# Loading one weight matrix in a single transfer: w_in as one load of 56 KB per partition instead of two of 28 KB

## The chip, the cores and the metric

The kernel runs on one core of one Trainium2 chip. The metric is the device time of one execution in microseconds (us), the median over several executions. Executions of one kernel mostly agree within 0.5 us. Differences of a few tenths of a us are therefore at the edge of what can be seen.

## The reference, cut to what matters

A decode step mixes two branches by a sigmoid gate: an attention with a long cache (4 key/value heads, 65,536 positions, head size 128), and a small gated MLP (here `B`) on one token.

```python
x = A_x                                        # 1 x 1 x 1024
g = sigmoid((x * gate_w).sum(-1))
a = attention(x @ wq, k_cache, v_cache) @ wo   # k_cache, v_cache: 4 x 65536 x 128 each, bf16
z = gelu(x @ w_in)                             # w_in: 1024 x 3584
z1, z2 = z[:1792], layernorm(z[1792:])
b = (z1 * (w_sp * z2 + b_sp)) @ w_out          # w_sp, b_sp: one number each
out = g * a + (1 - g) * b
```

All weights and the cache are read once, 162 MB in bf16. `w_in` is 7.34 MB of that.

## The kernel before: what the change touches

All large loads go into one SBUF buffer, `kv`, of five slots of 32 KB per partition, and all are issued by SyncE on one queue, in the order of use. `load` issues one transfer into the slot `at`; a slot is loaded again when its readers have finished. The very first load is moved ahead of the start-up barrier by a helper that is left out here.

```python
P = 128; CT = 128; NKV = 5                      # slot: CT * P elements of bf16 = 32 KB per partition
kv = big.tile([P, NKV * CT * P], BF16, name="kv")

def load(src, shape, at):                       # at: slot number
    ...                                         # n: elements of one partition
    v = kv[:, int(at * CT * P):int(at * CT * P) + n]
    ...
    ins = nc.sync.dma_start(out=v, in_=src)
    return v

# four small loads on ScalarE's queue: x and gate_w (8 rows of 256 B each), w_sp, b_sp (2 B each)
nc.scalar.dma_start(out=xg8[:, 0, :], in_=A_x...)
nc.scalar.dma_start(out=xg8[:, 1, :], in_=gate_w...)
nc.scalar.dma_start(out=wb[:, 0:1], in_=B_w_sp)
nc.scalar.dma_start(out=wb[:, 1:2], in_=B_b_sp.unsqueeze(0))

KH = KC // 2                                    # KC = 8 rows of w_in and wq per partition
win_view = B_w_in.rearrange("(p c) n -> p c n", c=KC)
win_t = [load(win_view[:, i * KH:(i + 1) * KH, :], (KH, F), 3 + i) for i in range(2)]
wq_view = A_wq.rearrange("(p c) n -> p c n", c=KC)
wq_t = [load(wq_view[:, i * KH:(i + 1) * KH, :], (KH, HD), 1 - i) for i in range(2)]
...
# PE: xb_ps (x and gate to columns), small_ps (gate, w_sp, b_sp), then z, tot_ps, q:
for i in range(2):
    x_rows(z_ps, win_t[i], ZN, i)               # 32 matmuls 128x448 for each half
...                                             # DVE: gelu, layernorm sums -> tot_ps -> uT
for i in range(2):
    x_rows(q_ps, wq_t[i], HN, i)                # 32 matmuls 128x512 for each half
...                                             # DVE: q, build_w
build_w(0)
for j in range(NT):                             # first K tiles go to slots 2, 1, 0, 3
    k_tile(0, j, load_kv(A_k_cache, 0, j, (2, 1, 0, 3)[j])[0])
    ...
project(load(B_w_out..., (FC, D), 4), FC, uT, 0, first=True)
...                                             # K and V loads of 64 KB per partition, in turn
for j, n, at in ((0, 2, 1), (2, 1, 3), (3, 1, 4)):   # the last V loads
    ...
...                                             # wo in six loads, the last two of 2 KB per partition
```

On PE, z comes after `small_ps`, which waits for b_sp; and q comes after `tot_ps`, which waits for z's work on DVE. The trace shows PE keep to that order: w_in's first half had landed at 11.12 us, but z began at 12.66, after the `small_ps` matmuls on b_sp at 12.15. The K load into slot 1 waits for q's first half (done at 32.94 us, the issue at 32.99), the one into slot 0 for its second half.

## Time and profile before

| | before |
|---|---|
| median time | 383.22 us (383.17 to 383.25, 3 runs) |
| read | 162.0 MB, mean 425 GB/s |
| busy: PE, DVE | 61%, 57% of the span |
| packets of the load queue | 4324 |

From the page of the kernel before: the span, the busy time of the engines, the busy share of the DMA engines and their rate in 40 equal slices, the packets by queue (packets, MB, share of the span of 16 engines), and the chain that ended last by engine. (PE is TensorE's matmuls, PEld its weight loads, DVE VectorE, ACT ScalarE, POOL GpSimd, SP SyncE; a q after a name is the engine's sequencer, L167 is line 167 of the kernel, x32 a count of instructions. A slice of the span is 9.5 us long.)

```profile
span 381.4 us, 2581 instructions
PE 232.4 (61%) x1372; PEld 56.8 (15%) x796; DVE 218.4 (57%) x211; ACT 39.6 (10%) x55; POOL 4.4 (1%) x10
...
DMA  9999999999999999999999999999999999999995
GB/s 376 439 426 416 433 436 440 436 461 429 400 426 440 440 435 426 440 440 440 440 428 440 440 440 433 428 427 406 433 440 428 426 433 427 440 411 436 440 405 230
DMA packets 4375, 162.17 MB, mean 425 GB/s; under 512 B 520, under 2 KB 524, under 8 KB 908
...
q1 hardware_dynamic: 4324, 162.01, 98.7%
q8 instruction: 8, 0.13, 0.1%
...
DMA 59%; PE 20%; DVE 16%; issue 2%; ACT 1%; SPq 1%; DVEq 0%; ACTq 0%
```

The DMA engines are at 90% or more in every slice but the last. The load queue (q1) alone takes 98.7% of what 16 engines could give. No compute engine is near that. Note queue q8, whose kind is "instruction": eight instruction fetches of 16 KB (0.13 MB), counted as 0.1% of the same 16 engines; they come up again later.

The timeline of the load queue (start in us, duration of the issue, what is issued; the very first w_in load, at 0.00 us, lies before this window):

```profile
0.79 0.33 SPq L167 DMA_DIRECT2D kv<-in_B_w_in_dram  x1
1.16 0.97 SPq L167 DMA_DIRECT2D kv<-in_A_wq_dram  x2
6.87 0.33 SPq L167 DMA_DIRECT2D kv<-in_A_k_cache_dram  x1
32.99 0.33 SPq L167 DMA_DIRECT2D kv<-in_A_k_cache_dram  x1
42.77 0.81 SPq L167 DMA_DIRECT2D kv<-in_A_k_cache_dram  x2
```

And the timeline of the engines at the start (start, duration, engine, line, what, how often, and in brackets how long the engine was idle before and for whom):

```profile
9.13 0.37 PE L233 MATMUL xb_ps<-xg,spread 8*128 8x256 bf16 x1 [9.13 <-DMA xg<-in_gate_w_dram]
11.94 0.16 DVE L249 CAST wbf<-wb 1x2 f32<-1x2 bf16 x1 [1.00 <-DMA wb<-in_B_b_sp_dram]
12.66 3.17 PE L277 MATMUL z_ps<-kv,xT 128*32 128x448 bf16 x32
19.67 3.07 PE L277 MATMUL z_ps<-kv,xT 128*32 128x448 bf16 x32 [3.84 <-DMA kv<-in_B_w_in_dram]
27.57 0.56 PE L316 MATMUL tot_ps<-rs,ones_f 128*128 128x2 f32 x2 [4.83 <-DVE rs L314]
29.39 3.55 PE L277 MATMUL q_ps<-kv,xT 128*32 128x512 bf16 x32 [1.26 <-DMA kv<-in_A_wq_dram]
39.12 3.61 PE L277 MATMUL q_ps<-kv,xT 128*32 128x512 bf16 x32 [6.18 <-DMA kv<-in_A_wq_dram]
48.83 8.89 DVE L384 STREAM_TRANSPOSE kv<-kv 128x2048 int32<-128x2048 int32 x4 [1.59 <-DMA kv<-in_A_k_cache_dram]
59.84 2.31 DVE L384 STREAM_TRANSPOSE kv<-kv 128x2048 int32<-128x2048 int32 x1 [2.12 <-DMA kv<-in_A_k_cache_dram]
```

Read it from the bottom up: DVE waits for K, q waits for wq, z's second half waits for w_in. Each of them waits for the stream of loads. Three pieces of the chain of waits (start, duration, what) show how deep the queue is:

```profile
197.63 25.93 DMA kv<-in_A_k_cache_dram
...
347.00 31.88 DMA kv<-in_A_wo_dram
378.92 0.43 PE out_ps L478 x3
```

The K load issued at 197.63 us is 8.39 MB and needs 19 us at 440 GB/s, but it lands after 25.93 us: other loads are ahead of it (the last of them, a V load, landed at 204.19 us). The last output weights land at 378.88 us and only PE, ScalarE and the store of the result follow.

### The profile page before, as it was taken

The page shows a single profiled execution, that of the slowest core. Times are in us where ns is not written, and L with a number is a line of the kernel's source. Part 1 is how long each engine was busy: PE and PEld are TensorE (multiplying, and loading weights), DVE is VectorE, ACT ScalarE, POOL GpSimd, SP SyncE. Part 2 cuts the span into 40 slices and gives each one's busy share as a digit, 9 for nine tenths or more (in the row PEclk, how much of TensorE's full clock was granted, in tenths as well). Part 3 has the DMA queues.
Part 4 walks back from the last instruction along what each step waited for, and adds up shares of the span by engine and source line. Part 5 has one row for each costly group of instructions (what it writes and reads, how often), then busy time and mean ns, then how long its engine had stood idle before and what let it go on. Part 6 is the DMA issues. An engine that isn't in the chain of part 4 may idle for free.

```text
span 381.4 us, 2581 instructions
## 1 busy us (share of the span) xinstructions
PE 232.4 (61%) x1372; PEld 56.8 (15%) x796; DVE 218.4 (57%) x211; ACT 39.6 (10%) x55; POOL 4.4 (1%) x10
## 2 busy tenths in 40 slices
PE   0433467678157944796397629872967196849355
PEld 0110011112011210121011101120111011212123
DVE  4241487996687506966977059669780488550040
ACT  1010001111601100114010001050001010500000
POOL 4000000000000000000000000000000000000000
PEclk9966659998759895989588959895799679969766
DMA  9999999999999999999999999999999999999995
GB/s 376 439 426 416 433 436 440 436 461 429 400 426 440 440 435 426 440 440 440 440 428 440 440 440 433 428 427 406 433 440 428 426 433 427 440 411 436 440 405 230
DMA packets 4375, 162.17 MB, mean 425 GB/s; under 512 B 520, under 2 KB 524, under 8 KB 908
## 3 DMA queue, kind: packets, MB, share of 16 engines
q1 hardware_dynamic: 4324, 162.01, 98.7%
q8 instruction: 8, 0.13, 0.1%
q14 instruction: 3, 0.02, 0.0%
q10 hardware_dynamic: 40, 0.01, 0.0%
HBM read 162.01 MB, written 0.00 MB: 425 GB/s over the span
## 4 chain that ended last, share of the span: by engine, by line
DMA 59%; PE 20%; DVE 16%; issue 2%; ACT 1%; SPq 1%; DVEq 0%; ACTq 0%
DMA kv<-in_A_k_cache_dram 37%; PE s_ps L391 15%; DVE kv L384 9%; DMA kv<-in_A_wo_dram 8%; DMA kv<-in_A_wq_dram 7%; DMA kv<-in_A_v_cache_dram 7%; PE o_ps L437 3%; DVE pt L427 2%; DVE mx L386 1%; DVE o_sb L451 1%; PE q_ps L277 1%; ACT sc L424 1%; DVE rowt L447 1%; ACT sc L402 1%; SPq L167 1%
## 5 line engine op out<-in xcount | busy, mean ns | idle before, releaser
L391 PE MATMUL s_ps<-kv,wt 128*128 128x512 bf16 x512 | 142.1, 437 | 81.8 <-DVE kv L384 81.7
L384 DVE STREAM_TRANSPOSE kv<-kv 128x2048 int32<-128x2048 int32 x64 | 142.7, 2280 | 55.5 <-DMA kv<-in_A_k_cache_dram 55.5
L437 PE MATMUL o_ps<-kv,pt 128*64 128x512 bf16 x512 | 61.6, 399 | 7.7 <-DMA kv<-in_A_v_cache_dram 7.7
L391 PEld LDWEIGHTS <-wt 128*128 128x128 bf16 x256 | 27.5, 108 | 197.6 <-issue 140.2
L402 ACT CAST sc<-s_ps 128x1024 bf16<-128x1024 f32 x16 | 16.2, 1013 | 253.5 <-PE s_ps L391 253.5
L437 PEld LDWEIGHTS <-pt 128*64 128x64 bf16 x256 | 16.0, 115 | 50.7 <-issue 48.1
L427 DVE STREAM_TRANSPOSE pt<-sc 128x1024 bf16<-128x1024 bf16 x16 | 18.6, 1217 | 6.8 <-ACT sc L424 6.8
L386 DVE TENSOR_REDUCE mx<-sc 128x1 f32<-128x1024 bf16 x12 | 14.5, 1207 | 10.1 <-ACT sc L402 10.1
L424 ACT ACTIVATE sc<-sc,nb 128x1024 bf16<-128x1024 bf16 x16 | 18.2, 1137 | 12.2 <-DVE nb L420 12.2
L447 DVE TENSOR_TENSOR rowt<-o_ps,own 128x1024 f32<-128x1024 f32 x4 | 4.8, 1194 | 24.9 <-PE o_ps L437 24.9
L457 PE MATMUL om_ps<-o_sb,hsel 128*32 128x128 f32 x8 | 2.5, 421 | 19.7 <-DVE o_sb L451 19.7
L406 DVE TENSOR_REDUCE mx<-sc 128x1 f32<-128x1024 bf16 x4 | 4.9, 1220 | 14.2 <-ACT sc L402 14.2
L277 PE MATMUL q_ps<-kv,xT 128*32 128x512 bf16 x64 | 7.2, 627 | 7.4 <-DMA kv<-in_A_wq_dram 7.4
L478 PE MATMUL out_ps<-kv,oa 128*32 128x256 bf16 x128 | 6.7, 366 | 3.7 <-DMA kv<-in_A_wo_dram 2.2
L277 PE MATMUL z_ps<-kv,xT 128*32 128x448 bf16 x64 | 6.2, 570 | 3.8 <-DMA kv<-in_B_w_in_dram 3.8
L344 DVE TENSOR_TENSOR rowt<-q_ps,own_b 128x512 f32<-128x512 f32 x2 | 1.3, 686 | 12.5 <-PE q_ps L277 12.5
L451 DVE TENSOR_REDUCE o_sb<-rowt 128x128 f32<-128x1024 f32 x4 | 7.5, 1872 | 0.1
L292 DVE TENSOR_TENSOR rowt<-z_ps,own_b 128x448 f32<-128x448 f32 x2 | 1.2, 620 | 8.5 <-PE z_ps L277 8.5
L233 PE MATMUL xb_ps<-xg,spread 8*128 8x256 bf16 x1 | 0.4, 367 | 9.1 <-DMA xg<-in_gate_w_dram 9.1
L277 PEld LDWEIGHTS <-xT 128*32 128x32 bf16 x64 | 3.0, 139 | 19.4 <-issue 19.3
L478 PEld LDWEIGHTS <-oa 128*32 128x32 bf16 x128 | 4.4, 124 | 6.1 <-issue 3.3
L521 ACT CAST out_sb<-out_ps 128x256 bf16<-128x256 f32 x1 | 0.4, 372 | 45.4 <-PE out_ps L478 45.4
(88 smaller groups left out, 54.8 us busy)
## 6 DMA issues: line engine op xcount, KB each, us to landing
kv<-in_A_k_cache_dram SPq DMA_DIRECT2D x4, 4096.0 KB, 26.8
kv<-in_A_wq_dram SPq DMA_DIRECT2D x2, 4096.0 KB, 32.8
kv<-in_A_v_cache_dram SPq DMA_DIRECT2D x2, 4096.0 KB
kv<-in_B_w_in_dram SPq DMA_DIRECT2D x2, 3584.0 KB, 15.0
kv<-in_A_wo_dram SPq DMA_DIRECT2D x1, 4096.0 KB
kv<-in_B_w_out_dram SPq DMA_DIRECT2D x1, 3584.0 KB
kv<-in_A_wo_dram SPq DMA_DIRECT2D x1, 2048.0 KB, 28.6
kv<-in_A_wo_dram SPq DMA_DIRECT2D x1, 1024.0 KB, 30.7
```

What stands on the lines that cost most here:

```text
L277: ins = nc.tensor.matmul(ps[t * B:(t + 1) * B, k * HN:k * HN + n], lhsT=xT[:, i * KH + c:i * KH + c + 1].to_broadcast([P, B]), rhs=w[:, c, ...
L384: nc.vector.transpose(out=kb[:, v * n:(v + 1) * n], in_=kb[:, v * n:(v + 1) * n])
L386: nc.vector.reduce_max(**late.pop())
L391: ins = nc.tensor.matmul(s_ps[:, k * HN:(k + 1) * HN], lhsT=wt[g % 2][:, v, b].rearrange("p a v h -> p (a v h)"), rhs=kx[:, b // 2, b % 2, ...
L402: nc.scalar.copy(out=sct[g, j][:], in_=s_ps[:])
L406: nc.vector.reduce_max(**late.pop())
L424: nc.scalar.activation(out=sct[g, j][:], in_=sct[g, j][:], func=ACT.Exp, scale=SCALE, bias=nb[:, 0:1], accum_out=lss[g][:, j:j + 1])
L427: nc.vector.transpose(out=ptt[g, j][:].rearrange("p c x -> p (c x)"), in_=sct[g, j][:])
L437: ins = nc.tensor.matmul(o_ps[g][hs, e, :], lhsT=ptt[g, j][:, 2 * u:2 * u + 2, :].rearrange("p c x -> p (c x)"), rhs=vx[:, 2 * u + e], sta ...
L447: nc.vector.tensor_tensor(out=om8, in0=o_ps[g][:].rearrange("p e (v d) -> p (e v) d", d=DH), in1=own_8[:].unsqueeze(2).to_broadcast([P, 2 ...
L451: nc.vector.tensor_reduce(out=o_sb[:], in_=om8.rearrange("p x d -> p d x"), axis=AX.X, op=ALU.add)
L478: nc.tensor.matmul(out_ps[t * B:(t + 1) * B, :], lhsT=vec[:, c0 + c:c0 + c + 1].to_broadcast([P, B]), rhs=w[:, c, t * NO:(t + 1) * NO], st ...
```

## The change

w_in goes into two neighbouring slots in any case, so its two loads can be one: 56 KB in one row per partition. The intent is fewer and larger transfers; the two loads were of 3.67 MB each.

```diff
     KH = KC // 2
     win_view = B_w_in.rearrange("(p c) n -> p c n", c=KC)
-    win_t = [load(win_view[:, i * KH:(i + 1) * KH, :], (KH, F), 3 + i) for i in range(2)]
+    win = load(win_view, (KC, F), 3)
+    win_t = [win[:, i * KH:(i + 1) * KH, :] for i in range(2)]
     wq_view = A_wq.rearrange("(p c) n -> p c n", c=KC)
```

The order of instructions on every engine stays as it was, apart from the one load less on SyncE.

## The prediction

> **What bounds the kernel now.** The stream of loads. The page shows the DMA engines at 90% or more in every slice but the last, 162.0 MB read at 425 GB/s in the mean; full slices reach 440. DVE is busy 57%, PE 61%. The chain of waits is DMA for 59%; its PE and DVE parts lie between a load's issue and the freeing of its slot. They are not the limit, because new loads find others ahead of them: in the timeline of the load queue the K load issued at 197.63 us lands 25.93 us later, and its 8.39 MB alone need 19 us at 440 GB/s. Some 5 us of queue stand between a late issue and an idle engine. The last output-weight load lands at 378.88 us, 2.5 us before the end.
>
> **What the change does.** The same 7.34 MB go to the same partitions. 128 row packets of 28 KB and 16 semaphore packets fall away[...]. One SyncE issue goes (0.36 us, timeline), but the queue was full then. Later loads move to the next completion semaphore; the first K load no longer waits for the small x load (to 6.87 us, for nothing the stream needed).
>
> *Gain.* 32 KB rows arrive at about 432 GB/s (wq: 4.19 MB in 9.7 us), 64 KB rows at up to 440: some 20 ns per packet and engine (my estimate from these rates). 8 rows fewer per engine give 0.1 to 0.2 us.
>
> *Cost.* All z matmuls must wait for the whole w_in, about 19.5 us, when the second half lands now; the first 32 (3.17 us, at 12.66 us) no longer run early. And the small loads share the engines with w_in. [...]x lands at 6.87 us, gate_w at 9.10, 2.2 us apart, two 28 KB packets (1.08 us each at 425/16 GB/s). With 56 KB packets I expect twice the delay: first matmul (xb_ps) at 14–17 us rather than 9.13, b_sp at 20–23 rather than 11.9, so z ends at 26–29 rather than 22.74. The tot_ps matmul, 4.8 us later, runs at 31–34 rather than 27.57, and q's first half slips from 29.39 to 32–35 us.
>
> *On the critical path?* No. wq's second half lands at 39.1 us, and q, build_w and the first K transpose (48.8 us) hang on that; the slip fits before it. The K load into slot 1, issued at 33 us after q's first half, goes out at 35–39, with wq's second half and the first K tile (until 48.8) still queued. DVE then waits 2.1 us for K, to 59.81, which would absorb a small slip.
>
> **Prediction.** 383.1 us, 8 in 10 between 382.4 and 383.7. Faster by over 2%: 0.01; within 2%: 0.98; slower: 0.01.
>
> **What would show it.** Right: xb_ps and z later, q's second half still at 39 us, first K transpose near 48.8, the K wait ending near 59.8, packets down by 144 to about 4231, last output-weight landing within 0.5 us. Wrong: q's second half or the first K transposes later, or DMA slices before 60 us below those of now.
>
> **What would make it wrong.** If b_sp lands beyond 23 us, q and the first K tiles slip, and with less queue left than I think the slip reaches the end. If large packets feed the engines better at the start, where 2 to 6 us shows 345 to 387 GB/s, up to 1 us could be won.

## The result, and the profile after

| | before | after |
|---|---|---|
| median time | 383.24 us (383.09 to 383.29, 6 runs) | 383.07 us (382.83 to 383.19, 6 runs) |
| ratio | | 0.9995, 95% interval 0.9983 to 1.0008 |
| packets, all queues | 4375 | 4231 |

A ratio is the mean time of one kernel's fast runs over that of the other's in the same rounds, so it is not quite the ratio of the medians quoted. The interval includes 1: the change is neutral, with a hint of 0.17 us.

From the page of the kernel after:

```profile
span 381.3 us, 2579 instructions
PE 230.5 (60%) x1372; PEld 56.4 (15%) x796; DVE 218.4 (57%) x211; ACT 39.6 (10%) x55; POOL 4.4 (1%) x10
...
DMA  9999999999999999999999999999999999999995
GB/s 385 440 433 416 423 429 440 440 485 429 407 412 419 440 442 433 433 433 440 440 428 440 440 440 440 435 434 399 419 440 435 426 440 427 426 414 433 437 412 225
DMA packets 4231, 162.17 MB, mean 425 GB/s; under 512 B 504, under 2 KB 508, under 8 KB 892
...
q1 hardware_dynamic: 4180, 162.01, 98.7%
q8 instruction: 8, 0.13, 0.1%
```

The timeline of its load queue (the one w_in load, at 0.00 us, again lies before the window):

```profile
0.80 0.82 SPq L167 DMA_DIRECT2D kv<-in_A_wq_dram  x2
1.68 0.46 SPq L167 DMA_DIRECT2D kv<-in_A_k_cache_dram  x1
35.28 0.33 SPq L167 DMA_DIRECT2D kv<-in_A_k_cache_dram  x1
42.57 0.80 SPq L167 DMA_DIRECT2D kv<-in_A_k_cache_dram  x2
```

The timeline of its engines:

```profile
13.20 0.37 PE L234 MATMUL xb_ps<-xg,spread 8*128 8x256 bf16 x1 [13.20 <-DMA xg<-in_gate_w_dram]
19.54 0.16 DVE L250 CAST wbf<-wb 1x2 f32<-1x2 bf16 x1 [4.53 <-DMA wb<-in_B_b_sp_dram]
20.27 6.03 PE L278 MATMUL z_ps<-kv,xT 128*32 128x448 bf16 x64
31.13 0.56 PE L317 MATMUL tot_ps<-rs,ones_f 128*128 128x2 f32 x2 [4.83 <-DVE rs L315]
31.62 3.61 PE L278 MATMUL q_ps<-kv,xT 128*32 128x512 bf16 x32
38.92 3.61 PE L278 MATMUL q_ps<-kv,xT 128*32 128x512 bf16 x32 [3.69 <-DMA kv<-in_A_wq_dram]
48.63 8.89 DVE L385 STREAM_TRANSPOSE kv<-kv 128x2048 int32<-128x2048 int32 x4 [1.59 <-DMA kv<-in_A_k_cache_dram]
59.45 2.31 DVE L385 STREAM_TRANSPOSE kv<-kv 128x2048 int32<-128x2048 int32 x1 [1.93 <-DMA kv<-in_A_k_cache_dram]
```

And from its chain of waits:

```profile
197.61 25.61 DMA kv<-in_A_k_cache_dram
...
347.03 31.79 DMA kv<-in_A_wo_dram
378.86 0.43 PE out_ps L479 x4
```

One issue is earlier: the first K load goes out at 1.68 us and not at 6.87, since it no longer waits for the small x load (before, both had semaphore 100, and x's eight updates of it ended at 6.85 us; after, the K load has semaphore 110), but w_in and wq are queued ahead of it in both kernels. Everything else up to q's first half is later: the first matmul by 4.07 us, the b_sp scalar by 7.60 us, the end of z by 3.56 us, the K load into slot 1 by 2.29 us. From q's second half on, all of it is gone: that half starts when wq has landed, at 38.92 us, and the K tiles come 0.2 to 0.4 us earlier than before. Not much hangs on these tenths: in `one_again` below, the same kernel, that half of q started at 39.05 us. The last output weights land 0.06 us earlier than before; one execution can't be read more finely than that. The prediction named two more marks for the start. The first six slices, up to 57 us, have a mean of 421 GB/s in both kernels, so the stream did not become thinner there; and in the first 10 us both moved 367 GB/s in the mean, so that nothing was won there, either.

### What the packet records add

The trace also has a record of every packet: start, duration, bytes and queue, but not which of the 16 engines served it. The large loads show one packet per row of a partition, and 16 packets of 4 bytes per load, the semaphore writes. (In the kernel before, those of w_in's first half end at 10.23 to 10.77 us of the span, and the trace has 16 updates of that load's semaphore by a DMA, at 10.58 to 11.12 us, each about 0.35 us later. x and gate_w, of 8 rows each, have 8 such packets and 8 updates each.) On the load queue the 144 packets less are rows of 28 KB, 384 to 128, rows of 56 KB, 0 to 128, and packets of 4 bytes, 482 to 466. Median duration of one packet of the load queue, in both kernels:

```
bytes      4     4096   8192   16384   28672            32768   57344          65536
ns         9     161    313    614     1062 / 1066      1216    2116 (after)   2421
```

From 4 KB to 64 KB this is a straight line: 11 ns for each row plus 0.0368 ns for each byte (27.2 GB/s per engine). So a row saved is worth 11 ns and not the 20 ns that I had estimated from arrival rates. With 8 rows and one semaphore packet less, an engine saves 8 x 11 + 9 = 97 ns. The sum of all packet times on the load queue, divided by 16, is 376.58 us before and 376.38 after, 0.20 us less; the rest of it lies mostly in the first rows of each engine, which are slow in both kernels (up to 2.2 us for a row of 28 KB, up to 3.2 us for one of 56 KB) and add a little less with one load.

And the small loads on ScalarE's queue, start of their packets in us after the first row of w_in began:

```
                x rows       x sems       gate rows    gate sems      w_sp   sem    b_sp   sem
two of 28 KB    3.86-4.40    4.94-5.47    6.01-6.54    7.08-7.61      8.29   9.35   9.36   10.43
one of 56 KB    4.83-5.30    6.96-7.42    9.07-9.54    11.20-11.67    13.61  15.73  17.85  17.86
```

A small packet waited for one row of w_in: the steps are 1.07 us with rows of 28 KB and 2.12 us with rows of 56 KB, and such a row lasts 1.062 and 2.116 us in the median. (In two places two small packets went out back to back: w_sp's semaphore and b_sp with 28 KB, b_sp and its semaphore with 56 KB.) So the row was the unit of the wait in both kernels.

### The profile page after: what moved, and what is told of

Read it like the earlier page. It is cut to its first block, busy times and chain, and to the rows that moved or that the text cites. A ratio compares the mean times of both kernels' runs of the same rounds, so it can differ in the third digit from the quotient of the medians.

```text
span 381.3 us, 2579 instructions
## 1 busy us (share of the span) xinstructions
PE 230.5 (60%) x1372; PEld 56.4 (15%) x796; DVE 218.4 (57%) x211; ACT 39.6 (10%) x55; POOL 4.4 (1%) x10
## 2 busy tenths in 40 slices
DMA packets 4231, 162.17 MB, mean 425 GB/s; under 512 B 504, under 2 KB 508, under 8 KB 892
## 4 chain that ended last, share of the span: by engine, by line
DMA 57%; PE 24%; DVE 14%; ACT 2%; issue 1%; SPq 1%; DVEq 0%; ACTq 0%
DMA kv<-in_A_k_cache_dram 42%; PE s_ps L392 20%; DMA kv<-in_A_wo_dram 8%; DVE kv L385 8%; DMA kv<-in_A_v_cache_dram 7%; PE o_ps L438 3%; DVE pt L428 2%; DVE o_sb L452 1%; DVE mx L387 1%; ACT sc L403 1%; ACT sc L425 1%; SPq L167 1%; DVE rowt L448 1%; PE om_ps L458 0%; DVE osum L468 0%
## 5 line engine op out<-in xcount | busy, mean ns | idle before, releaser
L392 PE MATMUL s_ps<-kv,wt 128*128 128x512 bf16 x512 | 140.3, 432 | 83.8 <-DVE kv L385 83.8
L438 PEld LDWEIGHTS <-pt 128*64 128x64 bf16 x256 | 16.1, 115 | 50.6 <-issue 48.1
```

Source lines behind the costliest of these rows:

```text
L392: ins = nc.tensor.matmul(s_ps[:, k * HN:(k + 1) * HN], lhsT=wt[g % 2][:, v, b].rearrange("p a v h -> p (a v h)"), rhs=kx[:, b // 2, b % 2, ...
L438: ins = nc.tensor.matmul(o_ps[g][hs, e, :], lhsT=ptt[g, j][:, 2 * u:2 * u + 2, :].rearrange("p c x -> p (c x)"), rhs=vx[:, 2 * u + e], sta ...
```

## The experiments

Theory A: the load stream is the limit; the late z lies in slack; the packets that fall away are worth 0.1 to 0.2 us. Rivals: B, nothing happens at all; C, the late z costs a few tenths and the packets pay for it; D, the small loads land late because of the amount of data ahead of them and not because of the size of the packets. All kernels gave right results. Unless said otherwise an edit starts from the kernel after the change.

### one_again: the changed kernel once more, five rounds

> The changed kernel again, to size a gain of a few tenths of a us. Theory A (the load stream is the limit, and 144 packets less save it 8 rows of about 20 ns per engine): 0.1 to 0.2 us below the kernel before, ratio 0.9995. Rival B (no gain, no cost; the difference seen is noise): within 0.05 us of the kernel before.

Measured: 383.11 us (383.09 to 383.16) against 383.27 (383.16 to 383.32), ratio 0.9997, interval 0.9984 to 1.0009. The difference has the predicted sign and size a second time, 0.16 us, but the interval still includes 1. One run can't tell A from B; the sweep of packet counts at the end of this section does more.

### z_twice and z_four: z made later still

```diff
-    for i in range(2):
+    for i in (0, 1) * 2:          # z_four: * 4
         x_rows(z_ps, win_t[i], ZN, i)
```

> The one load, with the 64 z matmuls done twice over (the second pass begins its sums anew, so the result is right). The late z is made 6.0 us later still. Theory A (slack): q's first half ends at about 41 us rather than 35.2, the K load into slot 1 goes out then, before the loads ahead of it are through (first K tile lands at 48.6), so nothing runs dry: 383.1, within 0.3 us of the one-load kernel. Rival C (late z costs some tenths of a us on the chain and the smaller packet count pays for it): a further 6 us of lateness shows as +0.3 us or more.

Measured: 383.27 us, 1.0001 (0.9988 to 1.0015). The second pass took only 2.3 us and not 6, so z ended 2.3 us later, and q's first half then started at 33.87 us rather than 31.62. So q's first half was done at 37.5 us, still before wq's second half landed. The first K transpose slipped from 48.63 to 50.08 us and the next wait for K ended at 59.79: absorbed. That slip is not the late z's, however. q's second half waited for wq, as before, and wq itself landed later:

```profile
40.37 2.49 PE L278 MATMUL q_ps<-kv,xT 128*32 128x512 bf16 x32 [2.88 <-DMA kv<-in_A_wq_dram]
```

That is 1.45 us later than with one load, and the next experiments give the reason: an instruction fetch, here at 30.0 us after the first row. The rise of 0.16 us in the time is smaller than C's 0.3, but the dose was smaller too.

> The same with z done four times: z ends at about 44.4 us, q's first half at about 53, 18 us later than with one load. Theory A: the queue has emptied at about 46.6 us (the first K tile lands at 48.6[...]), so the stream stands still for about 6.5 us until the K load into slot 1 is issued at about 53, and nothing gives that back: 389 to 397, the upper part if DVE, which starts some 14 us late, uses up the later slack too. If the time stays within 1 us of the one-load kernel, the stream isn't the limit and theory A falls; if it grows by the full 18 us, there was no slack.

Measured: 384.26 us, 1.0027 (1.0013 to 1.0041). This met neither text. The four passes took 14.05 us and not 24, so the K load into slot 1 went out at 43.16 us, before the queue was empty: no standstill was to be expected at this dose. (The 46.6 us in the text was too early as well: in the changed kernel the last row ahead of that load ends at 48.1 us, 0.5 us before the K tile's first transpose.) But 1.15 us more than `one_again` needed an explanation, and it is not at the start: even the last V load landed as it did in the changed kernel. The timeline of PE in `z_four`, near the end:

```profile
359.11 6.57 PE L438 MATMUL o_ps<-kv,pt 128*64 128x512 bf16 x32 [6.09 <-DMA kv<-in_A_v_cache_dram]
...
380.06 0.41 PE L479 MATMUL out_ps<-kv,oa 128*32 128x256 bf16 x4 [0.24 <-DMA kv<-in_A_wo_dram]
```

With the one load the same two lines start at 359.15 and 378.86 us. So the last V tile was on time and the last output weights came 1.2 us late. A late z can't do that 310 us after the fact without showing in between.

### pe_filler, filler_third, before_filler: instruction fetches

Theory F: passes of z are PE instructions, and those are fetched in packets of 16 KB (mostly 1.0 to 1.1 us each in the packet records) by the same DMA engines: the page of `z_four`, with 288 PE instructions more, has nine packets on q8 instead of eight. If a load is complete only when the slowest engine has finished, a fetch that is served late by an engine that is behind anyway moves the end. Theory L: the lateness of z is to blame after all.

```diff
+    fill_ps = psm.tile([P, 2], FP32, name="fill_ps", tag="m")
+    for n in range(96):           # filler_third: 32
+        for k in range(2):
+            ins = nc.tensor.matmul(
+                fill_ps[:B, k:k + 1], lhsT=wt[0][...][:, :B], rhs=wt[1][...0:1],
+                start=True, stop=True, skip_group_check=True)
+            if k > 0:
+                same_weights(ins)
     xb_ps = psm.tile([P, 2 * P], FP32, name="xb_ps", tag="m")
```

> Doing z four times cost 1.15 us, but all of it after 359 us (the V loads still landed at the times of the one-load kernel), so lateness of z is not the likely cause. Theory F (fetches): z four times adds 288 PE instructions, these come in one more packet of 16 KB (9 instead of 8 on the instruction queue), and the packet that comes at 375 us is now served by the engine that is last in any case; the last load ends when that engine ends, 1.1 us later. This run adds 288 PE instructions (192 matmuls of one column into a PSUM tile that nobody reads, 96 weight loads) while PE idles before x has landed, so z is hardly later. Theory F: 9 fetch packets, and 383.9 to 384.4 if the last one meets a late engine again, 383.1 if it meets an early one. Theory L (the lateness of z costs the time): 383.1, with the ends of the last rows together as in the one-load kernel.

Measured: 384.11 us, 1.0026 (1.0010 to 1.0041). z ran from 20.57 to 25.88 us, not later than with the one load, and yet the time is that of `z_four`. L falls. From the page of `pe_filler`, the fetches, and from its timeline z and the last matmuls:

```profile
q8 instruction: 9, 0.15, 0.2%
...
20.57 5.31 PE L286 MATMUL z_ps<-kv,xT 128*32 128x448 bf16 x64 [0.31 <-DMA kv<-in_B_w_in_dram]
...
379.80 0.41 PE L487 MATMUL out_ps<-kv,oa 128*32 128x256 bf16 x4 [0.24 <-DMA kv<-in_A_wo_dram]
```

> The one w_in load with 96 idle PE instructions (64 matmuls, 32 weight loads) before x has landed, as many as doing z twice added. Theory F (an instruction fetch that meets the last engine near the end costs about 1 us): with this count the ninth fetch packet falls at about 377 us or later, when the loads are through, as it did with z twice: 383.0 to 383.4. If the time goes with the count of PE instructions instead (288 cost 0.9 us), 383.4 to 383.5, and if any ninth packet costs 1 us, 384.1.

Measured: 383.26 us, 1.0000 (0.9987 to 1.0014). There are nine fetches here as well, but the packet records have the ninth at 377.0 us after the first row, when the loads are practically through (with z twice at 377.1). So a ninth fetch alone costs next to nothing; it matters when it comes.

> The kernel before the change (two w_in loads) with the 288 idle PE instructions. Theory F says that this cost has nothing to do with how w_in comes: the same ninth fetch packet near 373 us, 384.0 to 384.4. If the time stays near 383.2, the cost belongs to the one-load kernel's order of packets.

Measured: 384.55 us, 1.0033 (1.0020 to 1.0047), slightly above the range. The cost is there with two loads of w_in, too, so it has nothing to do with the change.

The same shows early on in these runs. Where a fetch ran before wq was through (at 25.2 to 33.9 us after the first row in `z_twice`, `filler_third`, `pe_filler` and `before_filler`), wq's second half landed at 40.26 to 40.55 us; without one (the kernel before, the one load twice, `four_loads`) at 38.92 to 39.25. (`short_rows`, with 40.12 us, is set apart: its whole stream runs a us late.) So with such a fetch the load ended 1.0 to 1.6 us later. The later slack absorbs this; at the end of the stream there is none.

The packet records, times in us from the first row of w_in (the 15th engine is the last row that doesn't belong to the engine that ends last):

```
kernel          fetches   last fetch at   15th engine done   16th engine done   load-queue time / 16
before          8         373.2           377.33             377.36             376.58
one load        8         372.8           377.14             377.33             376.38
z_twice         9         377.1           377.27             377.59             376.48
filler_third    9         377.0           377.31             377.31             376.44
z_four          9         373.5           377.27             378.58             376.41
pe_filler       9         372.3           377.33             378.31             376.41
before_filler   9         372.1           377.46             378.78             376.64
```

In the three slow ones the mean work per engine is unchanged and 15 engines are through at the usual time, but one ends 1.0 to 1.3 us after all others. The records don't name the engines, but a chain can be put together backwards from the last row, because packets follow each other closely (from the 4-byte packets of w_in's last load to those of wq's first half took 9.68 us in the kernels before and after, and eight rows of 32 KB and one packet of 4 bytes last 9.74 us in sum), so that each can be taken to start within 20 ns of the end of the one before, and the order of the rows is known. Over the last five loads the chain of the last engine in `z_four`, `pe_filler` and `before_filler` closes only if the late fetch is put into it; in the kernel with one load, in `one_again`, `z_twice` and `filler_third` it closes without a fetch only, and in the kernel before both ways. So theory F is what the runs support: 288 PE instructions that delay nothing cost 0.9 to 1.3 us, 96 cost nothing that can be told from noise, and in each costly case the fetch sits on the engine that ends last.

The same records say why nine fetches cost and eight don't. Followed back to the first row of w_in, every chain of the last engine that closes in the three slow kernels holds two fetches; in `z_four` a single chain closes, with the first fetch (28.8 us) and the ninth. In the kernel before, the one load twice, `z_twice` and `filler_third`, every chain holds at most one. This did not depend on the gap allowed between packets (from 18 ns of overlap and 15 ns of gap to 40 and 30). And a fetch costs its engine more than its own 1.0 to 1.1 us: in these eight kernels the row or two rows that follow it (the first starts up to 16 ns before the fetch ends) take 0.46 to 0.55 us longer than others of their size, for all 67 fetches that have rows after them. So one fetch takes about 1.5 us from its engine, and an engine that has served two ends after all others. A ninth fetch at 377 us comes when the rows are through and does no harm. Why the ninth goes to an engine that has had one already is not recorded; that the lengthening comes back after eight fetches (in `z_four` 465, 478, 547, 546, 491, 495, 504, 465 ns, then 461) would fit eight engines that take turns; this is my estimate from these nine numbers, and no record shows it.

### z_eight: is there a loss once the slack is used up?

> z done eight times, since four passes took only 14.05 us (a further pass is 2.8 us, not 6) and so made q's first half end at about 43 us, still before the queue is empty at about 46.6. Eight passes: z ends at about 45.6 us, q's first half at about 54. Theory A (slack, then loss): the stream stands still for 7 to 8 us, the first K tiles' successors land that much later, and the time is 390 to 393 (up to 1 us of it from further instruction fetches). If the time stays within 2 us of 383.1, a dry queue costs nothing and A falls.

Measured: 393.26 us (392.37 to 394.12), 1.0263 (1.0244 to 1.0282), just above the expected range. From the busy table by stretches of `z_eight` (stretch, its length, busy us and instructions of PE, weight loads, DVE, ACT and POOL, granted clock, DMA share, GB/s):

```profile
44.00:48.00 4.00, 2.59 (x56) 0.59 (x24) 1.31 (x3) 0.00 (x0) 0.00 (x0) 1.00 0.90 381
48.00:52.00 4.00, 0.57 (x6) 0.53 (x6) 2.88 (x10) 1.51 (x2) 0.00 (x0) 0.94 0.04 16
52.00:56.00 4.00, 4.00 (x52) 0.88 (x24) 1.56 (x8) 0.20 (x1) 0.00 (x0) 0.63 0.00 0
56.00:60.00 4.00, 1.01 (x21) 0.20 (x5) 2.80 (x4) 0.00 (x0) 0.00 (x0) 1.00 1.03 393
```

The DMA engines stand still for eight us, from 48 to 56 us, until the K load into slot 1 goes out at 55.31 us. That is the loss: the stretch from the first to the last row grew from 377.33 to 386.54 us, 9.2 us, and the work per engine by 0.4. So the stream is the limit (A), and the queue of loads ahead of slot 1 lasts until about 48 us. The changed kernel issues that load at 35.28 us, 12.7 us before that; about one of these us passes from an issue to its first rows (55.31 to 56.27 us here), and the first engine runs out of rows at 47.5 us, so 10 us or more of slack are left, and the change used 2.29. Of the ten us in the time, eight are the standstill; the rest is not traced.

### short_rows: one load, but in small packets

```diff
-    win = load(win_view, (KC, F), 3)
+    win = kv[:, 3 * CT * P:5 * CT * P].rearrange("p (a b) -> p a b", a=KC)[:, :, :F]
+    first_load.append(nc.sync.dma_start(out=win, in_=win_view).ins.name)
```

> w_in still in one load, but into rows of 8 KB pitch in SBUF, so that it moves in 1024 packets of 7 KB instead of 128 of 56 KB; count of loads, waits and instructions stay. It tells apart what the size of packets does from what the number of loads does. Theory A[...]: the small loads land far earlier than with one load of 56 KB packets: first matmul (xb_ps) at 3.5 to 6 us rather than 13.2, the b_sp scalar at 4 to 7 rather than 19.5; z from about 19.5 us. Rival D (the small loads land late because of the bytes or the single load ahead of them): xb_ps stays beyond 9 us. For the time: at 20 ns a packet, 56 packets more per engine cost 1.1 us (384.2); if packets cost next to nothing, 383.1.

Measured: 384.17 us, 1.0025 (1.0012 to 1.0039). From its timeline:

```profile
7.19 0.37 PE L235 MATMUL xb_ps<-xg,spread 8*128 8x256 bf16 x1 [7.19 <-DMA xg<-in_gate_w_dram]
...
20.67 2.81 PE L279 MATMUL z_ps<-kv,xT 128*32 128x448 bf16 x28 [10.45 <-DMA kv<-in_B_w_in_dram]
```

One load with the same 7.34 MB ahead, and the first matmul runs at 7.19 us instead of 13.20: D falls, it is the size of the packets. But 7.19 is later than the 3.5 to 6 I expected: the first small packet is served 3.6 us after the first row here, too (3.86 with 28 KB rows). That part grew far less than the rows (3.6 us at 7 KB, 3.86 at 28 KB, 4.83 at 56 KB). The time, 1.06 us above `one_again`, is what 20 ns per row would give, but by luck, for it is made of other terms: the first row starts 0.39 us later (1.41 us after the issue against 1.02; the issue itself takes 0.65 us rather than 0.40), and the stretch from the first to the last row is 0.65 us longer. For the 56 rows more per engine, 11 ns each would be 0.62 us (the 7 KB rows take 275 ns in the median, which is 11 ns plus the bytes).

### four_loads: the other way

```diff
-    win = load(win_view, (KC, F), 3)
+    KQ = KC // 4
+    win_q = [load(win_view[:, i * KQ:(i + 1) * KQ, :], (KQ, F), 3 + i * KQ * F / (CT * P))
+             for i in range(4)]
+    win = kv[:, 3 * CT * P:3 * CT * P + KC * F].rearrange("p (a b) -> p a b", b=F)
```

> w_in in four loads of 14 KB per partition, the other way from the change. Theory A with 11 ns a row and 9 ns a semaphore packet: against one load 24 rows and 3 semaphore packets more per engine, 0.29 us: 383.3 to 383.5. [...]the rows take about 0.54 us each, so x, gate and the two scalars land at about a half of the delay they have with 28 KB rows: first matmul at 5.5 to 7 us (9.13 with two loads, 13.2 with one), the scalar b_sp at 7 to 9 us.

Measured: 383.51 us, 1.0008 (0.9994 to 1.0021), at the upper end of the range; first matmul at 7.14 us, a little late again by that part, and b_sp was used at 8.87 us. The small packets stand 0.54 us apart here.

### wq_one and wq_v_one: merging more loads

wq becomes one load of 64 KB rows as well (q's second half is then computed first, so that slot 1 comes free early), and in `wq_v_one` the last two V loads, too.

```diff
-    wq_t = [load(wq_view[:, i * KH:(i + 1) * KH, :], (KH, HD), 1 - i) for i in range(2)]
+    wq = load(wq_view, (KC, HD), 0)
+    wq_t = [wq[:, i * KH:(i + 1) * KH, :] for i in range(2)]
...
-    for i in range(2):
-        x_rows(q_ps, wq_t[i], HN, i)
+    for i in (1, 0):                            # x_rows: start and stop by the first half done
+        x_rows(q_ps, wq_t[i], HN, i, first=1)
...                                              # wq_v_one only:
-    for j, n, at in ((0, 2, 1), (2, 1, 3), (3, 1, 4)):
+    for j, n, at in ((0, 2, 1), (2, 2, 3)):
```

> w_in in one load, and wq in one load of 64 KB per partition too; q's second half is computed first, so that slot 1 comes free after half of the matmuls. Theory A: 144 packets less again; the packet records give about 11 ns for a row and 9 ns for a semaphore packet, so 8 rows and one such per engine are 0.1 us: 383.0. q now starts when all of wq has landed at 38.9 us and ends 3.5 us later than with two loads (about 46), the K load into slot 1 goes out at about 42.7 us, before the queue is empty at 46.6; the first K transpose comes at about 52 rather than 48.6. If that slip is not absorbed: 383.5 or more.

Measured: 383.07 us, 0.9996 (0.9984 to 1.0009). The 64 matmuls of q took 4.97 us from 38.70, so the K load into slot 1 went out at 41.99 us and the first K transpose slipped less than expected, to 49.57 us.

> As the run with one wq load, and the last two V loads of 32 KB rows as one of 64 KB rows: 144 packets less again. Theory A: a further 0.1 us, 382.9, unless the last V tile, which now lands with the one before it, delays the output-weight load into its slot. The end of the last rows decides: below 0.3 us from the kernel with the one w_in load in either direction.

Measured: 382.78 us (382.69 to 383.05), 0.9991 (0.9979 to 1.0004): the fastest kernel, but the interval still includes 1. It lies 0.33 us from the kernel with one load, a little outside the 0.3 of the text.

Put side by side by the number of packets (medians of five rounds, before in the same rounds 383.19 to 383.27; for the kernel before, the 383.24 us of its six runs):

```
kernel        packets   us        load-queue time / 16 engines
short_rows    5128      384.17    377.26
four_loads    4663      383.51    376.73
before        4375      383.24    376.58
one load      4231      383.11    376.40
wq_one        4087      383.07    376.22
wq_v_one      3943      382.78    376.19
```

Both columns fall from line to line, by about 0.15 us for 144 packets in the mean of the lower four. The intervals of one load, `wq_one` and `wq_v_one` all include 1; that all three lie on the same side is what speaks for A against B. It isn't proof. The medians are from three sets of rounds; against the kernel before in the same set, `four_loads`, one load, `wq_one` and `wq_v_one` stand at +0.27, -0.16, -0.12 and -0.41 us, so the step from one load to `wq_one` is not resolved, and the last two kernels change waits as well as packets. A little more weight for a gain comes from the single executions in the rounds of `one_again`: the slowest of five with one load (383.16) is no slower than the fastest of nine of the kernel before (383.16).

## Why the prediction was right

- **The limit.** The stream of loads is the limit. Shown by `z_eight`: eight us without DMA cost about ten, and supported by `z_twice` and `filler_third`, where more PE work in the slack cost at most 0.2 us.
- **The late z is off the critical path.** Shown in the profile after: the slip of 2 to 8 us ends at q's second half, which starts at 38.92 us because wq lands then. The slack left at the K load into slot 1 is 10 us or more. C has no support: its sign of life, `z_four`, was caused by the number of PE instructions (`pe_filler`).
- **The gain.** Predicted 0.1 to 0.2 us, seen as 0.17 and 0.16 us in the medians of two sets of runs. Each alone is within the noise. That the number fits so well is partly luck: half of the 0.20 us less work per engine lies in the slow first rows, which the prediction did not name, and makes up for the rows' smaller cost.
- **The term that was mis-sized: a row.** The estimate was 20 ns for a packet; the packet records give 11 ns. The saving by rows is 0.10 us rather than 0.16.
- **The term that was mis-sized: the delay of the small loads.** "With 56 KB packets I expect twice the delay" gave 14 to 17 us for the first matmul and 20 to 23 for b_sp; 13.20 and 19.54 were measured, and q's first half started at 31.62, ahead of the 32 to 35 expected. Only the steps between small packets double (1.07 to 2.12 us); the 3.9 to 4.8 us until the first of them is served don't. z's end (26.3 us), tot_ps (31.13) and the issue into slot 1 (35.28) fell into their ranges.
- **The other marks.** 4231 packets were predicted and counted. First K transpose 48.63 (near 48.8), K wait ending at 59.45 (near 59.8), last output weights 0.06 us from before, GB/s before 60 us not below those of the kernel before.
- **What the prediction had not seen.** The stream ended with its slowest engine, and a second instruction fetch on one engine moved that end by about 1 us, more than the change itself: in the three slow kernels 15 engines were through at 377.27 to 377.46 us and the last at 378.31 to 378.78. That the change left the PE instructions alone is why this did not show.

## What to carry to other kernels

Here one queue of loads kept the DMA engines busy from end to end (90% or more in 39 of 40 slices), and merging two loads that were already some MB each saved little: about 0.1 us for 128 rows and their semaphore writes, and 0.1 us in the first rows. Work that became late was free because the load into the slot it held went out (at 35.28 us) before the queue ran dry (from 47.5 us in `z_eight`), so compute that moment first. Large rows had a side effect: a small load on another queue waited for one whole row per packet (1.07 us at 28 KB, 2.12 us at 56 KB), so small loads on which much depends are better beside small rows, as in `four_loads` (0.54 us); issuing them before the large rows was not tried. And when a time differs by about a us for no visible reason, count the instruction-fetch packets before blaming the edit: here the ninth cost 0.9 to 1.3 us when it came before the last rows, on an engine that had served one already.
